# Attention of eight batches and an MLP on one core: later AV products, a third u buffer, early MLP products, and keys split by DMA

The chip is one Trainium2 chip, of which the kernel uses **one core**. The metric is the device time of one execution in microseconds (us), as the median of several executions. The word *span* is the time from the first to the last instruction in one profiled execution; in every execution of this case the device time was 1.7 to 1.8 us above its span.

## The reference, cut to what matters

```python
# q, k, v: (8 batches, 8 heads, 576 positions, 64); bias_table: (32, 8)
scores = scale * np.matmul(q, k.transpose(0, 1, 3, 2)) + bias     # bias by distance and head
attn = softmax(scores)                                            # over the keys
x = np.matmul(attn, v).transpose(0, 2, 1, 3).reshape(4608, 512)
h = x @ w_in                                                      # 512 -> 2048
s = np.sin(alpha * h)
g = h + s * s / (alpha + 1e-09)
out = g @ w_out                                                   # 2048 -> 512
```

The kernel works batch by batch (t = 0 to 7). It computes the attention of a batch, two heads ("a pair", p = 0 to 3) at a time, and then one block of 512 tokens of the MLP, whose second half is slipped between the next batch's scores.

## The kernel before: the parts that matter

A scheduler written in Python places "tasks" on the engines at build time. A task has possible engines, predecessors, buffers and a priority (a lower number goes first); an engine then runs its instructions in the order in which they were placed. `NBUF` holds the number of buffers of each kind, and `u` is the exponentials of one pair.

```python
NBUF = {"sc": 4, "av": 2, "mo": 2, "u": 2, "g": 2, "s16": 3, "sq": 3, "outs": 5, "xn": 3}
AV_PRI = 250
# ... (cut)
def load_kqT(t):                      # batches 2 to 7; all of it in SyncE's queue
    nc.sync.dma_start_transpose(out=kraw[:, :, :], in_=staged_k.ap()[t])
    kz = kzs[t % 2]
    nc.sync.dma_start(out=kz[0:64, :, 0:S], in_=kraw[0:64, :, :])
    nc.sync.dma_start(out=kz[64:128, :, S : 2 * S], in_=kraw[64:128, :, :])
    for z in range(2):
        r = slice(64 * z, 64 * z + 64)
        nc.sync.dma_start(out=kts[t % 2][r, :, r], in_=kraw[r, :, 512:S])
    nc.sync.dma_start_transpose(out=qTs[t % 2][:, :, :], in_=staged_q.ap()[t])
# ... (cut)
def plan_tr(t, p, kq, pri, nb, deps=()):    # batches 0 and 1: TensorE transposes a pair
    # ... (cut: transposition into a PSUM buffer c.v of kind "mo")
    def cp(e):                              # copies on VectorE or ScalarE
        if kq == 1:
            put(qTs[t][:, p, :], slice(0, 128))
        else:
            put(kzs[t][:, p, 0:S], slice(0, 64))
            put(kzs[t][:, p, S : 2 * S], slice(64, 128))
    def tail(e):                            # "corners": keys 512 to 575 of both heads
        for z in range(2):
            r = slice(64 * z, 64 * z + 64)
            nc.vector.tensor_copy(
                out=kts[t][r, p, r], in_=kzs[t][r, p, S * z + 512 : S * z + S])
# ... (cut)
def first(t=t):                             # called at the first score of batch t
    if 1 <= t < T - 1:
        load_v16(t + 1)
        load_kqT(t + 1)
    if t + 2 < T:
        stage_kq(t + 2)
```

`kz` holds a pair's keys with the other head's half left at zero, so that a product over 128 rows gives one head alone; `kt` holds the last 64 keys of both heads. `kraw` is the place where a transposed batch lands before it is spread to `kz` and `kt`. There is one `kraw`.

The softmax here doesn't subtract the row's maximum and nothing guards it: scores larger than these inputs give would overflow.

## Time and profile before

| | before |
|---|---|
| median of 3 executions | 414.31 us (414.13 to 416.89) |
| profiled execution | 412.09 us, span 410.3 us |
| TensorE busy | 395.4 us, 96% of the span |
| ScalarE, VectorE busy | 337.3 and 289.7 us |

The kernel is bound by TensorE: its row of busy tenths is 9 from the fifth slice to the last but one. Only time in which TensorE waits or runs cold can be won.

### The profile page before, as it was taken

What the parts mean: (1) busy time and instruction counts of PE and PEld (TensorE: products, weight loads), DVE (VectorE), ACT (ScalarE), POOL (GpSimd) and SP (SyncE); (2) the same over time, 40 slices, a digit from 0 to 9 for tenths busy, and PEclk for the clock granted to TensorE, in tenths of its full rate; (3) what the DMA queues carried; (4) which work ended last, traced back from release to release, by engine and by line L of the source; (5) the groups of instructions that cost most, each with busy time, mean ns of one, the idle gap of its engine ahead of it and who ended that gap; (6) DMA issues with size and microseconds to landing.
All of it is one profiled execution on the core that took longest, in us unless ns stands there. A gap on an engine that the chain in (4) does not pass through costs nothing.

```text
span 410.3 us, 8747 instructions
## 1 busy us (share of the span) xinstructions
PE 395.4 (96%) x3519; PEld 227.5 (55%) x3519; DVE 289.7 (71%) x683; ACT 337.3 (82%) x502; POOL 85.6 (21%) x98
## 2 busy tenths in 40 slices
PE   4897999999999999999999999999999999999996
PEld 1474446754576447744665467645764477444442
DVE  5895996749666976688576956696768766799200
ACT  2877988879988998889888998799979988899311
POOL 7863952044000900071004400120000000000000
PEclk9999999999999999999999999999999999999999
DMA  9899999949900995099906990293000000000111
GB/s 170 189 206 219 205 162 158 216 89 164 185 28 29 155 182 94 27 135 165 131 28 104 161 142 27 69 169 79 27 28 27 26 27 27 28 1 0 53 77 77
DMA packets 135145, 41.90 MB, mean 102 GB/s; under 512 B 121209, under 2 KB 129489, under 8 KB 135105
## 3 DMA queue, kind: packets, MB, share of 16 engines
q0 software_dynamic: 89872, 19.04, 54.5%
q1 hardware_dynamic: 45008, 22.26, 24.2%
q8 instruction: 27, 0.44, 0.4%
q14 instruction: 14, 0.11, 0.1%
q10 hardware_dynamic: 224, 0.05, 0.1%
HBM read 37.76 MB, written 16.52 MB: 132 GB/s over the span
## 4 chain that ended last, share of the span: by engine, by line
PE 88%; DVE 8%; DMA 1%; ACT 1%; issue 1%; ACTq 0%; DVEq 0%
PE sc L408 44%; PE mo L408 30%; PE av L408 11%; PE av L688 2%; DVE kz L496 2%; DVE g L741 2%; DMA phi_sb<-phi_const 1%; DVE u L635 1%; DVE xn L678 1%; DVE qT L496 1%; ACT u L606 1%; DVE kt L542 1%; DVE sq L736 0%; PE mo L507 0%; PE mo L513 0%
## 5 line engine op out<-in xcount | busy, mean ns | idle before, releaser
L606 ACT ACTIVATE u<-sc 128x768 f16<-128x768 f32 (+1 forms) x224 | 165.9, 788 | 28.6 <-PE sc L408 23.5
L408 PE MATMUL mo<-w_out,g 128*128 128x512 f16 x576 | 156.5, 379 | 0.0
L408 PE MATMUL sc<-xT,w_in 128*128 128x512 f16 x576 | 131.2, 379 | 0.5 <-DVE g L741 0.5
L741 DVE SCALAR_TENSOR_TENSOR g<-sq,inv_a,sc 128x512 f16<-128x512 f16 x144 | 104.7, 747 | 7.8 <-ACT sq L734 4.9
L727 ACT ACTIVATE s<-sc,alphaT 128x512 f16<-128x512 f32 x144 | 92.4, 677 | 8.4 <-PE sc L408 7.3
L408 PE MATMUL sc<-qT,kz 128*128 128x192 f16 (+1 forms) x512 | 89.5, 288 | 2.0 <-ACT qT L494 0.7
L408 PEld LDWEIGHTS <-w_in 128*128 128x128 f16 x576 | 55.3, 98 | 64.7 <-issue 0.8
L635 DVE TENSOR_TENSOR u<-u,m2r 128x512 f16<-128x512 f16 (+1 forms) x192 | 70.5, 388 | 17.4 <-ACT u L606 14.9
L408 PEld LDWEIGHTS <-g 128*128 128x128 f16 x576 | 55.8, 98 | 45.2
L408 PEld LDWEIGHTS <-u 128*128 128x128 f16 x1440 | 55.2, 97 | 10.6 <-ACT u L606 2.5
L352 POOL DMA_DIRECT2D v<-in_v_dram x24 | 22.2, 1064 | 163.7 <-PE av L408 163.7
L408 PE MATMUL av<-v,u 128*128 128x65 f16 x1280 | 54.9, 193 | 0.5 <-DVE u L635 0.5
L408 PEld LDWEIGHTS <-kz 128*128 128x128 f16 x512 | 42.6, 98 | 22.0 <-issue 4.4
L734 ACT ACTIVATE sq<-s 128x512 f16<-128x512 f16 x79 | 49.4, 629 | 2.3
L677 DVE RECIPROCAL rd<-av 128x6 f32<-128x6 f32 x64 | 12.0, 188 | 38.1 <-PE av L408 38.1
L408 PE MATMUL av<-vh,u 128*128 128x130 f16 x160 | 35.2, 220 | 0.1
L678 DVE TENSOR_TENSOR xn<-av,rd 128x384 f16<-128x384 f32 x64 | 31.4, 491 | 2.2
L736 DVE TENSOR_TENSOR sq<-s 128x512 f16<-128x512 f16 x65 | 27.3, 421 | 2.9 <-ACT s L727 2.5
L496 DVE COPY outs<-mo 128x512 f32<-128x512 f32 x27 | 18.6, 690 | 10.9 <-PE mo L408 10.7
L688 PEld LDWEIGHTS <-xn 128*128 128x128 f16 x160 | 13.6, 98 | 18.0 <-DVE xn L678 6.4
L494 ACT ACTIVATE outs<-mo 128x512 f32<-128x512 f32 x9 | 5.4, 597 | 20.7 <-PE mo L408 20.7
L688 PE MATMUL av<-id_sb,xn 128*128 128x128 f16 x160 | 19.5, 220 | 2.9 <-DVE xn L678 2.8
(68 smaller groups left out, 185.6 us busy)
## 6 DMA issues: line engine op xcount, KB each, us to landing
out_dram<-outs SPq DMA_DIRECT2D x36, 256.0 KB, 2.0
staged_k<-in_k_dram POOLq DMA_DIRECT2D x6, 576.0 KB, 11.2
staged_q<-in_q_dram POOLq DMA_DIRECT2D x6, 576.0 KB, 17.5
kz<-kraw SPq DMA_DIRECT2D x12, 288.0 KB, 7.0
v<-in_v_dram POOLq DMA_DIRECT2D x24, 128.0 KB, 6.0
w_in<-in_moe_w_in_dram POOLq DMA_DIRECT2D x4, 512.0 KB, 8.5
w_out<-in_moe_w_out_dram POOLq DMA_DIRECT2D x4, 512.0 KB, 10.8
w_out<-in_v_dram SPq DMA_DIRECT2D x4, 256.0 KB, 9.1
```

Source lines behind the costliest of these rows:

```text
L352: nc.gpsimd.dma_start(out=vs[t % 2][:, c, :, 0:D], in_=vp[128 * c : 128 * c + 128],)
L408: nc.tensor.matmul(out=out, lhsT=lhsT, rhs=rhs, start=start, stop=stop)
L496: k_of(e).tensor_copy(out=o, in_=i)
L606: nc.scalar.activation(out=o, in_=x, func=AF.Exp, scale=0.125)
L635: nc.vector.tensor_tensor(out=io, in0=io, in1=m2[:, 2 * p : 2 * p + 2, x0 : x0 + hi - lo], op=ALU.mult,)
L677: nc.vector.reciprocal(out=r, in_=a[:, :, :, D])
L678: nc.vector.tensor_tensor(out=xn.v[:, 0:nq].rearrange("p c (z d) -> p c z d", z=2), in0=a[:, :, :, 0:D], in1=r.unsqueeze(3).to_broadcast([ ...
L688: nc.tensor.transpose(out=tr.v[:, qc - q0 : qc - q0 + 128], in_=xn.v[:, i], identity=id_sb)
L727: nc.scalar.activation(out=s16.v, in_=h.v, func=AF.Sin, scale=alphaT[:, f : f + 1])
L734: nc.scalar.activation(out=sq.v, in_=s16.v, func=AF.Square)
L736: k_of(e).tensor_tensor(out=sq.v, in0=s16.v, in1=s16.v, op=ALU.mult)
L741: nc.vector.scalar_tensor_tensor(out=gcell[b].v[:, f, :], in0=sq.v, scalar=inv_a[:, f : f + 1], in1=h.v, op0=ALU.mult, op1=ALU.add,)
```

## The change

The intent is to shorten the first 60 us, where TensorE waits for ScalarE and VectorE. It has three parts. **Part 1**: the AV products (exponentials times v) of batch 0 get a late priority, so that the next pair's scores go first, and `u` gets a third buffer (it shares its memory with `nat1`, where inputs of batch 0 are loaded). **Part 2**: the first MLP products are cut in two, so that three of four need not wait for the last pair. **Part 3**: keys of pairs 2 and 3 of batch 0 and of all pairs of batch 1 leave PSUM in one 128-partition copy to `kraw`, and four DMAs spread them from there. These DMAs go into SyncE's queue. The placing times `T_TR1` of batch 1's transpositions also change, from 38.5 and 38.5 to 33 and 37 (among the lines cut below).

```diff
-NBUF = {... "u": 2, ...}
+NBUF = {... "u": 3, ...}
-AV_PRI = 250
+AV_PRI = (2000, 250)
+FAR = 1
   ... (cut)
@@ plan_tr
+        far = kq == 0 and (t == 1 or p > FAR)
+            elif far:
+                put(kraw[:, p, :], slice(0, 128))
-        eng = {"DVE": 0.75, "ACT": 0.72} if kq else {"DVE": 1.6, "ACT": 1.55}
+        eng = {"DVE": 0.75, "ACT": 0.72} if kq or far else {"DVE": 1.6, "ACT": 1.55}
+        if far:
+            farq.append((p, x))
+            if t and p % 2 == 0:
+                return [], []
   ... (cut)
+            def split(e):
+                kz = kzs[t]
+                nc.sync.dma_start(out=kz[0:64, p0:p1, 0:S], in_=kraw[0:64, p0:p1, :])
+                nc.sync.dma_start(out=kz[64:128, p0:p1, S : 2 * S], in_=kraw[64:128, p0:p1, :])
+                for z in range(2):
+                    r = slice(64 * z, 64 * z + 64)
+                    nc.sync.dma_start(out=kts[t][r, p0:p1, r], in_=kraw[r, p0:p1, 512:S])
+            y = plan.add({"DMA": D_SPLIT}, split, [z[1] for z in ps_], pri)
@@ plan_av
-            prev = [plan.add({"PE": 0.31}, mm, us + prev, base + AV_PRI + i,
+            prev = [plan.add({"PE": 0.31}, mm, us + prev, base + AV_PRI[t > 0] + i,
@@ plan_moe_in
-            m = plan.add({"PE": 4 * t_pe(512)}, mm, xs, pri, nb=T_W if b == 0 else 0.0, new=[hb])
+            if b == 0 and f < 4:
+                m = plan.add({"PE": 3 * t_pe(512)}, lambda e, mm=mm: mm(e, range(3)), xs012,
+                             pri - 100, nb=T_W, after=qk_last[:], new=[hb])
+                m = plan.add({"PE": t_pe(512)}, lambda e, mm=mm: mm(e, range(3, 4)), xs + [m],
+                             pri, use=[hb])
+            else:
+                m = plan.add({"PE": 4 * t_pe(512)}, mm, xs, pri, new=[hb])
```

More of the change, by code (lines that the diff above doesn't have):

```diff
@@ L34 @@
 LAT = {"PE": 0.2, "ACT": 0.18, "DVE": 0.18, "POOL": 0.2, "DMA": 0.0}
-NBUF = {"sc": 4, "av": 2, "mo": 2, "u": 2, "g": 2, "s16": 3, "sq": 3, "outs": 5, "xn": 3}
+NBUF = {"sc": 4, "av": 2, "mo": 2, "u": 3, "g": 2, "s16": 3, "sq": 3, "outs": 5, "xn": 3}
 class Task:
@@ L94, in run @@
     def run(self, t0):
-        free = {e: t0 for e in ("PE", "ACT", "DVE", "POOL")}
+        free = {e: t0 for e in ("PE", "ACT", "DVE", "POOL", "DMA")}
         todo = list(self.tasks)
@@ L163 @@
 T_V = (18.5, 45.0)
-T_TR1 = (38.5, 38.5)
+T_TR1 = (33.0, 37.0)
+D_SPLIT = 3.5
 T_W = 30.0
@@ L172 @@
 SIN_SET = "trig_and_small"
-SLACK = {"PE": 0.02, "ACT": 0.02, "DVE": 0.02, "POOL": 0.02}
+SLACK = {"PE": 0.02, "ACT": 0.02, "DVE": 0.02, "POOL": 0.02, "DMA": 0.0}
 def _bucket_table(max_abs: int) -> np.ndarray:
@@ L282 @@
     nat2 = nat2x[0:SN, 0 : 2 * H * SI * D].rearrange("s (kq h x) -> s kq h x", kq=2, h=H)
-    nat1x = sgl.tile([128, 2 * (H - 2) * SI * D], F16, name="nat1")
-    nat1 = nat1x[0:SN].rearrange("s (kq h x) -> s kq h x", kq=2, h=H - 2)
+    ubs = [sgl.tile([128, 9 * S], F16, name=f"u{i}") for i in range(3)]
+    uit = [0]
+    nat1 = ubs[2][0:SN, 0 : 2 * (H - 2) * SI * D].rearrange("s (kq h x) -> s kq h x", kq=2, h=H - 2)
     def new_g():
@@ L289, in new_u @@
     def new_u():
-        return tp.tile([128, 9, S], F16, name="u", tag="u", bufs=NBUF["u"])
+        uit[0] += 1
+        return ubs[(uit[0] - 1) % 3].rearrange("p (c q) -> p c q", c=9)
     def new_xn():
@@ L496, in copy_on @@
             k_of(e).tensor_copy(out=o, in_=i)
+    farq, split_of = [], {}
     def plan_tr(t, p, kq, pri, nb, deps=()):
         b, c = Buf("mo"), Cell()
+        far = kq == 0 and (t == 1 or p > FAR)
         def mm(e):
@@ L537, in plan_tr @@
             return [x], [x]
+        if far:
+            farq.append((p, x))
+            if t and p % 2 == 0:
+                return [], []
+            ps_ = [y for y in farq]
+            farq.clear()
+            p0, p1 = ps_[0][0], ps_[-1][0] + 1
+            def split(e):
[6 more added lines that the diff above has]
+            y = plan.add({"DMA": D_SPLIT}, split, [z[1] for z in ps_], pri)
+            for z in ps_:
+                split_of[(t, z[0])] = y
+            return [y], [y]
         def tail(e):
@@ L563, in plan_alpha @@
         return plan.add({"DVE": 0.4}, cp, [m], 5000, use=[b])
+    qk_last = []
     def plan_pair(t, p, kqt, tails, first, gate, ub):
@@ L612, in plan_pair @@
             head = head or [m]
+            qk_last[:] = [m]
             x = plan.add({"ACT": t_act(n)}, ex, [m] + gate, base + 20, use=b + [ub])
@@ L709, in plan_moe_in @@
         gcell[b], gbuf[b] = Cell(), Buf("g")
+        xs012 = [d for w in range(2) for d in xdone[(0, w)][0 : NP - 1]]
         xs = [d for t in range(T) for w in range(2) for d in xdone.get((t, w), [])
@@ L715, in plan_moe_in, with mm @@
             h, s16, sq = Cell(), Cell(), Cell()
-            def mm(e, f=f, h=h):
-                h.v = new_sc(1)
-                for j in range(4):
+            def mm(e, js=range(4), f=f, h=h):
+                if js[0] == 0:
+                    h.v = new_sc(1)
+                for j in js:
                     full(
@@ L815 @@
             tails = tr[(t, p, 0)][1] if t < 2 else []
+            if (t, p) in split_of:
+                kqt, tails = kqt + [split_of[(t, p)]], []
             u, done = plan_pair(t, p, kqt + pe_gate, tails, first, gate, ub)
```

## The prediction

> **What bounds the kernel now.** I read the page first: shares, slices, and the chain that ended last.
>
> ```profile
> span 410.3 us, 8747 instructions
> PE 395.4 (96%) x3519; PEld 227.5 (55%) x3519; DVE 289.7 (71%) x683; ACT 337.3 (82%) x502; POOL 85.6 (21%) x98
> ...
> PE   4897999999999999999999999999999999999996
> ...
> PE 88%; DVE 8%; DMA 1%; ACT 1%; issue 1%; ACTq 0%; DVEq 0%
> ```
>
> TensorE fills nearly every slice, so only time in which it waits can be won. Adding up its matmuls from the built program (columns over 2.4 GHz plus 2.5 ns each) gives 384.9 us; some 25 of the 410.3 us are losses, most of them before 100 us. So next I read the busy time by stretch of 5 us (PE is the second number) and the timeline of ScalarE.
>
> ```profile
> 20.00:25.00 5.00, 4.34 (x67) 3.17 (x65) 4.90 (x15) 3.77 (x7) 5.00 (x8) 1.00 1.03 203
> ...
> 35.00:40.00 5.00, 3.15 (x56) 2.17 (x53) 2.19 (x7) 2.97 (x5) 1.51 (x2) 1.00 1.20 242
> ...
> 55.00:60.00 5.00, 4.48 (x21) 2.04 (x21) 4.88 (x14) 4.78 (x8) 1.74 (x1) 1.00 2.45 158
> ...
> 23.66 0.81 ACT L606 ACTIVATE u<-sc 128x768 f16<-128x768 f32 x1 [1.19 <-PE sc L408]
> ...
> 35.82 0.81 ACT L606 ACTIVATE u<-sc 128x768 f16<-128x768 f32 x1 [0.65 <-PE sc L408]
> ...
> 39.62 1.31 ACT L494 ACTIVATE kz<-mo 64x576 f16<-64x576 f16 x2
> 40.96 2.04 ACT L727 ACTIVATE s<-sc,alphaT 128x512 f16<-128x512 f32 x3
> ...
> 58.64 1.28 ACT L789 ACT_TABLE_LOAD   x1
> ```
>
> The first batch's attention ends near 39; its exponentials stop for TensorE (1.19 us when pair 2 needs a u buffer that pair 0's AV still reads). From 41 to 58.6 ScalarE and VectorE are both full: first MLP half, with batch 1's key copies in between. That is what the change is after. It also puts new work on the SyncE queue, so I read that queue's own timeline, and TensorE's where pair 2 of batch 1 starts:
>
> ```profile
> 57.81 5.83 SPq L340 DMA_TRANSPOSE kraw<-staged_k  x1
> 69.33 0.63 SPq L342 DMA_DIRECT2D kz<-kraw  x1
> 70.07 1.25 SPq L343 DMA_DIRECT2D kz<-kraw  x1
> 71.37 1.32 SPq L346 DMA_DIRECT2D kt<-kraw  x2
> 72.80 6.35 SPq L347 DMA_TRANSPOSE qT<-staged_q  x1
> 79.25 8.80 SPq L782 DMA_DIRECT2D out_dram<-outs  x4
> ...
> SPq L340 <- DMA staged_k<-in_k_dram: 44.2, 1, 44.2
> ...
> 72.49 0.81 PE L408 MATMUL sc<-qT,kz 128*128 128x384 f16 x4
> ```
>
> This is the load of batch 2: SyncE sits 44.2 us on the staged keys, and is not free for anything else until 79.25. Before, that harmed nobody.
>
> **What the Trainium skill says.** "DMA: Bandwidth & Descriptors", section on the anatomy of one DMA: DMA engines do not wait on semaphores; the wait is on the issuing sequencer, before dispatch. The trace agrees: the 44.2 us are SyncE's, and the key copies behind stay behind it. "TensorE: Matmul & The Clock Gate", Part 2 (step by step): only weight loads are pulled ahead, matmuls stay in program order; so a score that waits holds all later TensorE work. No wait before is long enough to show it. The same page, Part 1 (what's actually happening): after about 3.4 us idle the array is at 1.2 GHz, and warm again after some 3.4 us of work. The trace has the cold start: four 128x384 matmuls took 1.56 us at 10.14 and 0.82 us at 23.08.
>
> **The change, part by part.**
>
> 1. *Third u buffer, AV of batch 0 at a late priority.* In the built order TensorE now sends pair 2's scores before the last AVs of pair 0. It removes the ScalarE waits of 1.19, 0.74 (at 27.35) and 0.65: 2.6 us. Last exponential 36.63 - 2.6 = 34.0; the tail from there to the last xT copy took 39.57 - 36.63 = 2.9, so attention ends near 37.
>
> 2. *First MLP products without the last pair.* Nine of the first sixteen matmuls (at 0.216 us: 1.9 us) now lie in the AV tail. The two key copies on ScalarE (1.31 us) no longer stand before the first sine: it comes near 37.3 instead of 40.96, 3.6 us earlier.
>
> 3. *Keys through one 128-partition copy.* A pair cost two 64x576 copies of 0.76 us and two corner copies of about 0.18; now one 128x576 copy of 0.76 (same length: a qT copy of that shape took 0.76). In the MLP stretch of batch 0 this frees on VectorE 3 x 0.76 + 1.4 = 3.7 us and gives it two or three squares (0.4) in exchange; ScalarE's 17.7 us (40.96 to 58.64) falls to 16 sines at 0.67, 8 squares at 0.52 and 4 copies at 0.53 = 17.0. Gain 0.7. Parts 1 to 3: 4.3 us, so batch 1's scores begin near 55 instead of 59.13.
>
> 4. *The split by DMA, in the SyncE queue.* The built order of SyncE is: batch 1 pairs 0-1 split (four DMAs); transpose of batch 2's keys into kraw; four copies out of it; transpose of batch 2's queries; only then batch 1 pairs 2-3 split. TensorE's first weight load of batch 1 pair 2 waits for exactly that DMA (I compared semaphore and count in the built program). Timing from the lines above: staged keys landed at 57.8, SyncE free at 79.25. First half issued from 79.25, second to 80.5. Landing: the output DMA issued at 79.25 took 4.2 us, the key copies issued at 69 to 70 took 6.4 and 8.8; with half their bytes I take 5 for both, so 85. Two extra splits (0.33 MB each, at some 0.2 MB per us in a DMA system busy from 20 to 57) push the staged keys by up to 3 us; I take 1.5. Pair 2 can start at **86.5**.
>
> TensorE gets there far earlier: pairs 0-1 took 72.49 - 59.13 = 13.4, less the six second-MLP matmuls that the new order puts later (1.3), from 55: near 67. It **stands still about 19 us**. Parts 1 to 3 end before that and do not count at all: neither staging of batch 2 nor SyncE's transposes wait for them.
>
> 5. *From there to the end.* Before, 410.3 - 72.49 = 337.8 us for matmuls that sum to 330.9: 6.9 over. The new order has 333.5 us from this place (twelve more matmuls). 333.5 + 6.9 = 340.4. Everything after is TensorE-bound, with no slack to catch up. Cold clock: 3.4 to 4 us at half speed, 2 us lost.
>
> Sum: 86.5 + 340.4 + 2 = 428.9 span. The median of the timed runs was 4.0 above the profiled span (414.3 against 410.3); partly the profiled execution being quick itself (412.1). I take 3: **432 us**, 4% slower.
>
> The order also has a defect: batch 2's keys overwrite kraw before pairs 2-3 of batch 1 are read from it, so heads 4 to 7 of batch 1 see wrong keys. The scores are tiny; worked out on the host this moves the output by 0.35% in norm, which a tolerance will likely pass. It costs no time.
>
> **Rivals.**
>
> - *No stall; the change works as meant.* Then 410.3 - 4.3 = 406 span, 410 us, -1%. For it: such a stall would be glaring to whoever made the change, and its own scheduler counts a split as 3.5 us. Against: SyncE issues in order, and the same transposes occupied it to 79.25. For this the staged keys would have to land 20 us sooner; GpSimd stages them at 45.44, behind loads that the change does not touch.
> - *The split is late in batch 0 already.* kraw of pair 2 is copied near 16.3, four issues at about 0.65 us and 4 to 7 us of landing put it at 21 to 24; ScalarE wants it at 22.5. This can eat 1.5 of part 1's 2.6 us: 411 to 412 us without the stall, and nothing with it, as the stall's end is not set by TensorE.
> - *VectorE becomes the bound of batch 0's attention.* From 18.6 it has about 17.6 us of masks and norms, so ends no earlier than 36.2: parts 1 and 2 then give 3 us, not 3.6. Again hidden by the stall.
> - *The stall is shorter or longer.* Landing after 4.2 us, no delay of the staging, warm clock: 83.5 + 340.4 + 3 = 427. Delay 3.5, landings 8.8, cold for longer: 91.5 + 340.4 + 3 + 4 = 439.
>
> **Range and chances.** The last rival's ends, a little wider below as 6.9 may shrink: 425 to 439. Same needs the stall to be 10 us shorter than worked out: 5%. Faster needs both no stall and twice the gain: 1%.
>
> **What would show it.** Busy time by stretch: TensorE nearly idle from about 67 to 86, one wait of 15 to 20 us at a score matmul (the helper's line is 412 in the new kernel), put down to a DMA kz<-kraw; matmuls after it at double length for some 4 us and a PEclk digit below 9. SyncE's timeline: the split of kz at 79 to 82, right after the query transpose. Part 1: no ScalarE gap near 23. Part 2: first sine near 37. Part 3: no 64x576 copies after 20 us. It is wrong if pair 2 of batch 1 starts before 75; if it starts at 86 but the end is below 424, the rest was not TensorE-bound as I take it.

## The result, and the profile after

The changed kernel took **426.83 us** (425.97 to 427.34, 4 runs) and the kernel before, in the same rounds, 414.22 us (410.79 to 416.89, 4 runs). The ratio of the fast runs is 1.031, with a 95% interval of 1.023 to 1.039: slower. Here and below a ratio is the mean time of one kernel's fast runs over the mean of the other's fast runs of the same rounds, so it is not quite the ratio of the medians.

First the page of the changed kernel, with the same lines as in the prediction and the slices of the granted clock:

```profile
span 425.5 us, 8795 instructions
...
PE 395.3 (93%) x3518; PEld 227.7 (54%) x3518; DVE 285.7 (67%) x668; ACT 335.8 (79%) x499; POOL 86.0 (20%) x98
...
PE   6889982099999999999999999999999999999996
...
PEclk9999998589999999999999999999999999999999
...
PE 79%; DMA 14%; POOL 5%; issue 1%; ACT 0%; SPq 0%; POOLq 0%; ACTq 0%
```

TensorE is busy for as long as before (395.3 against 395.4 us), but the row of slices has a hole, 2 and 0, where before it was full. The clock row falls to 8 and 5 in these two slices and is 8 in the next, and the chain that ended last now runs through DMA for 14% of the span. So 15 us were added as waiting, not as work. The busy time by stretch of 5 us shows the hole (columns: the stretch, then busy time of TensorE, of its weight loads, of VectorE, ScalarE and GpSimd with counts, granted clock, DMA share, GB/s). First one stretch of the kernel before, where TensorE is full:

```profile
70.00:75.00 5.00, 5.00 (x72) 3.73 (x71) 3.77 (x12) 4.43 (x7) 0.00 (x0) 1.00 2.20 184
```

Then the changed kernel:

```profile
65.00:70.00 5.00, 1.77 (x37) 1.37 (x34) 1.67 (x6) 1.94 (x3) 0.33 (x1) 1.00 1.62 123
70.00:75.00 5.00, 0.00 (x0) 0.00 (x0) 0.00 (x0) 0.00 (x0) 0.00 (x0) 0.55 2.43 157
75.00:80.00 5.00, 0.00 (x0) 0.00 (x0) 0.00 (x0) 0.00 (x0) 0.00 (x0) 0.50 1.87 219
80.00:85.00 5.00, 0.72 (x2) 0.24 (x3) 0.00 (x0) 0.00 (x0) 0.00 (x0) 0.50 0.85 166
85.00:90.00 5.00, 5.00 (x40) 2.81 (x39) 1.64 (x5) 3.13 (x5) 0.00 (x0) 0.74 0.14 52
```

TensorE stands still from 66.8 us, VectorE and ScalarE from 68.2 and 67.6, and all of them until 84; GpSimd has nothing to do in this time either. TensorE's timeline says what it waited for (columns: start, length, engine, line, operation, and the idle time before with what ended it):

```profile
84.28 0.96 PE L412 MATMUL sc<-qT,kz 128*128 128x384 f16 x2 [17.51 <-DMA kz<-kraw]
85.04 1.49 PE L412 MATMUL mo<-w_out,g 128*128 128x512 f16 x3
...
93.18 0.81 PE L412 MATMUL mo<-w_out,g 128*128 128x512 f16 x3
```

One wait of 17.51 us, at a score of pair 2 of batch 1, for `kz<-kraw`. The three 128x512 products right after it take 1.49 us, and 0.81 us at 93.18: the cold clock. SyncE's own timeline shows why the DMA was late:

```profile
59.10 5.80 SPq L344 DMA_TRANSPOSE kraw<-staged_k  x1
...
75.01 6.33 SPq L351 DMA_TRANSPOSE qT<-staged_q  x1
81.39 0.60 SPq L557 DMA_DIRECT2D kz<-kraw  x1
...
84.04 20.76 SPq L822 DMA_DIRECT2D out_dram<-outs  x4
```

The splits (lines 557 to 561 of the new kernel) stand behind the load of batch 2: keys' transpose, four copies, queries' transpose. Issued at 81.39, the split landed after 2.85 us, and TensorE started.

ScalarE's timeline answers to the lines on parts 1 and 2:

```profile
21.02 4.42 ACT L637 ACTIVATE u<-sc 128x768 f16<-128x768 f32 x6 [0.72 <-PE sc L412]
...
37.35 1.84 ACT L761 ACTIVATE s<-sc,alphaT 128x512 f16<-128x512 f32 x3 [0.54 <-PE sc L412]
```

The gap of 1.19 us at 23.66 is gone, and the first sine comes at 37.35 instead of 40.96. Of these 3.6 us, 1.4 are chance: this execution's first exponential started at 9.66 instead of 11.09, since its first loads landed sooner. So about 2.2 us of gain were there, and the stall swallowed them.

### The profile page after: what moved, and what is told of

The parts are those of the page before. It is cut to its first block, busy times and chain, and to the rows that moved or that the text cites. A ratio compares the mean times of both kernels' runs of the same rounds, so it can differ in the third digit from the quotient of the medians.

```text
span 425.5 us, 8795 instructions
## 1 busy us (share of the span) xinstructions
PE 395.3 (93%) x3518; PEld 227.7 (54%) x3518; DVE 285.7 (67%) x668; ACT 335.8 (79%) x499; POOL 86.0 (20%) x98
## 4 chain that ended last, share of the span: by engine, by line
PE 79%; DMA 14%; POOL 5%; issue 1%; ACT 0%; SPq 0%; POOLq 0%; ACTq 0%
PE sc L412 40%; PE mo L412 28%; PE av L412 9%; DMA staged_q<-in_q_dram 8%; DMA v1st<-in_v_dram 4%; PE av L720 2%; POOL v L376 1%; DMA natx<-in_q_dram 1%; DMA kz<-kraw 1%; POOL w_in L391 1%; POOL kz L402 0%; POOL vh L379 0%; POOL kz L401 0%; POOL m2r L426 0%; POOL nat L386 0%
## 5 line engine op out<-in xcount | busy, mean ns | idle before, releaser
L412 PE MATMUL sc<-qT,kz 128*128 128x192 f16 (+1 forms) x512 | 90.7, 290 | 21.6 <-DMA kz<-kraw 17.9
L709 DVE RECIPROCAL rd<-av 128x6 f32<-128x6 f32 x64 | 12.1, 189 | 38.5 <-PE av L412 38.3
```

The costliest lines, as they stand in the source:

```text
L412: nc.tensor.matmul(out=out, lhsT=lhsT, rhs=rhs, start=start, stop=stop)
```

## The experiments

Two theories came first. **Theory Q (the queue)**: the loss is the place of batch 1's second split in SyncE's queue, and nothing else. **Rival L (the landing)**: the split by DMA is slow in itself, because it lands late, whatever its place. (The recorded texts call these theory A and rival B; their rival C is that the new order of TensorE costs time as well.) Later two questions followed: where the expected gain went once the stall is gone, and which part is worth what.

The table gives one row per kernel. Stages are read from ScalarE's timeline of the profiled execution, whose loads of the activation table mark the changes between exponentials and sines: attention 0 from the first exponential to the next load, MLP 0 from there to the load after, attention 1 from there to the load after that. "Load at" is the time of that last load; from there to the very last table load every kernel takes 262.6 to 265.3 us. One execution is one sample: the first exponential alone varies from 9.0 to 11.7 us.

| kernel | median us (range) | ratio to before, 95% | first exp. | attention 0 | MLP 0 | attention 1 | load at | span |
|---|---|---|---|---|---|---|---|---|
| before | 414.22 (410.79 to 416.89) | | 11.09 | 25.56 | 21.99 | 26.96 | 85.60 | 410.3 |
| after | 426.83 (425.97 to 427.34) | 1.031 | 9.66 | 23.95 | 20.32 | **45.38** | 99.31 | 425.5 |
| e1_load_after_split | 412.53 (408.41 to 414.60) | 0.995 (0.989 to 1.000) | 11.40 | 28.37 | 20.40 | 27.75 | 87.92 | 412.8 s |
| e2_queries_after_split | 424.19, one run | | 11.38 | 28.18 | 20.39 | 37.55 | 97.50 | 422.4 |
| e3_split_batch0_only | 418.16 (410.47 to 418.46) | none | 10.45 | 30.10 | 24.29 | 26.68 | 91.52 | 416.6 s |
| e4_no_split | 416.70 (410.19 to 417.67) | 0.996 (0.988 to 1.004) | 11.39 | 23.83 | **27.65** | 27.95 | 90.82 | 415.5 s |
| e8_corners_from_psum | 411.39 (409.09 to 411.86) | 0.992 (0.986 to 0.998) | 10.11 | 26.13 | 20.31 | 26.04 | 82.59 | 407.3 |
| e9_before_corners_from_psum | 416.64 (414.62 to 417.45) | 1.004 (0.999 to 1.010) | 11.72 | 27.08 | 21.91 | 27.65 | 88.36 | 414.8 |
| e10_no_split_corners_psum | 412.40 (411.20 to 415.62) | 0.996 (0.988 to 1.003) | 10.89 | 29.52 | 23.93 | 26.17 | 90.51 | 413.8 |
| e12_mlp_whole | 410.98 (409.87 to 411.65) | 0.991 (0.984 to 0.997) | 10.75 | 28.21 | 21.09 | 25.66 | 85.71 | 409.9 |
| e11_av_early | 411.01 (410.22 to 411.80) | 0.990 (0.986 to 0.994) | 9.61 | 29.24 | 20.28 | 26.49 | 85.62 | 409.0 |
| e13_split_pair3 | 415.91 (413.41 to 416.29) | 1.000 (0.996 to 1.005) | 9.03 | **34.41** | 20.84 | 26.18 | 90.46 | 414.0 |
| **e14_split_batch1_only** | **407.31** (405.43 to 408.58) | **0.981** (0.977 to 0.985) | 10.52 | 24.01 | 20.90 | 25.79 | 81.22 | 405.4 |
| e15_best_av_early | 409.28 (408.04 to 409.94) | 0.985 (0.980 to 0.989) | 11.20 | 26.59 | 20.01 | 25.07 | 82.87 | 407.8 |

An "s" marks a profiled execution that counted as slow, because it was over 1.5% above the fastest of its kernel. The kernel before ran 410.8 to 420.4 us in these rounds, so a single profile can flatter or harm a kernel by some us. The ratios rest on fast runs. For e3 all runs but one counted as slow and no ratio was given. The profiled executions of e1, e4 and e10 are among the slowest of their kernels, and that of e8 is its quickest (409.09). All outputs passed the comparison.

### e1: the same DMAs, another order

```diff
     def qk(e, ...):                       # scores of pair p of batch t
+        if t == 1 and p == 2:
+            load_kqT(2)
     def first(t=t):
-            load_kqT(t + 1)
+            if t > 1:
+                load_kqT(t + 1)
```

> The change as it is, but SyncE issues the load of batch 2's keys and queries after the split of batch 1's pairs 2-3, not before. Theory A (order of the SyncE queue): the same DMAs through the same queue, so the wait of 17.5 us at pair 2's first score falls under 1 us, PEclk stays full, span 404 to 407, time 407 to 410 us. Rival B (the split itself lands late because the DMA engines are busy): a wait of 5 us or more stays, span above 411. Rival C (the stall is only part of it, the new order of TensorE costs too): no wait, but span above 410.

SyncE's queue and the TensorE waits of this kernel:

```profile
59.66 0.59 SPq L557 DMA_DIRECT2D kz<-kraw  x1
...
71.65 6.07 SPq L344 DMA_TRANSPOSE kraw<-staged_k  x1
```

```profile
25.42 0.34 PE L412 MATMUL sc<-qT,kz 128*128 128x384 f16 x1 [1.85 <-DMA kz<-kraw]
...
27.01 0.34 PE L412 MATMUL sc<-qT,kz 128*128 128x384 f16 x1 [1.25 <-DMA kz<-kraw]
```

The split of batch 1 is issued at 59.66 in place of 81.39, the stall at its pair 2 is gone, and attention 1 falls from 45.38 to 27.75 us. No DMA was removed or shortened. That decides for theory Q on the 17.5 us. By the letter of the expectation, though, this is rival C's outcome: no wait there, but a span of the profiled execution of 412.8 us, far above what I expected. Its trace shows a second loss, in batch 0. TensorE waits there 1.85 and 1.25 us for the split of batch 0, whose key copies landed 7.5 and 8.6 us after issue, and attention 0 takes 28.4 us. In this execution the landing, rival L's point, is the loss of batch 0. The waits cost twice here, as the same kernel's busy time by stretches of 1 us shows (the clock is third from the end):

```profile
24.00:25.00 1.00, 0.00 (x0) 0.00 (x0) 0.86 (x3) 0.42 (x1) 0.47 (x1) 1.00 1.08 221
...
28.00:29.00 1.00, 1.00 (x9) 0.47 (x6) 0.44 (x2) 0.19 (x1) 0.76 (x1) 0.50 1.07 223
```

TensorE is idle at 24, still at full clock; at 28 it is busy, at half clock. From 27 to 31 the granted clock was 0.75, 0.50, 0.50 and 0.54, with TensorE always busy: 0.25 + 0.50 + 0.50 + 0.46 = 1.7 us lost on top of the 3.1 us of waits. In e8 below, waits of 0.30 and 2.20 us left the clock at 1.00.

The changed kernel has the same code in batch 0, and did not lose this: its profiled execution took 23.95 us there. Its split went out sooner and landed sooner (after 5.4 and 5.0 us). First the changed kernel, then e1:

```profile
14.63 0.53 SPq L557 DMA_DIRECT2D kz<-kraw  x1
```

```profile
17.84 0.53 SPq L557 DMA_DIRECT2D kz<-kraw  x1
```

So the split of batch 0 can be late, and in some executions is not. The new order also mends a defect: in the changed kernel batch 2's keys overwrite `kraw` before the split of pairs 2 and 3 of batch 1 has read it.

### e2: half of the queue moved

```diff
 def load_kqT(t):
     # ... keys as before
-    nc.sync.dma_start_transpose(out=qTs[t % 2][:, :, :], in_=staged_q.ap()[t])
+    if t != 2:
+        load_qT(t)                        # batch 2: called at pair 2 of batch 1
```

> The change, but of batch 2's load only the transpose of the queries is issued after the split; the keys' transpose and copies stay before it. Theory A: the split is issued 6.3 us sooner (75 instead of 81.4), so the wait at pair 2 is about 11 us instead of 17.5 and the span about 419. If what counts were the landing of something else (staged keys, load of the DMA engines), the wait would not move by this amount. The order of the keys is still wrong, so heads 4 to 7 of batch 1 are off as in the change.

```profile
75.50 0.63 SPq L561 DMA_DIRECT2D kz<-kraw  x1
...
79.46 2.99 SPq L355 DMA_TRANSPOSE qT<-staged_q  x1
```

```profile
81.25 0.83 PE L416 MATMUL sc<-qT,kz 128*128 128x384 f16 x2 [8.46 <-DMA kz<-kraw]
```

With only the queries' transpose taken from ahead of it, the split is issued 5.9 us earlier (75.50), as theory Q wants. TensorE starts 3.0 us earlier (81.25 against 84.28), not 5.9: the split now takes 5.5 to 5.7 us to land, probably because other transfers run beside it (157 GB/s from 75.0 to 75.5 us), where it took 2.85 us in the quiet end of the stall (68 GB/s from 80 to 81 us). No run tests that. The shorter wait of 8.46 us is partly due to TensorE arriving later. So the dose has the right sign, and less than its full size.

### e3 and e4: which split, and none

```diff
-        far = kq == 0 and (t == 1 or p > FAR)
+        far = kq == 0 and t == 0 and p > FAR      # e3: batch 0 alone
+        far = False                               # e4: no split; parts 1 and 2 stay
```

> The change with the split by DMA in batch 0 alone; batch 1's keys are copied by VectorE and ScalarE in two halves as before. Theory A: no long wait, span 406 to 408 (some 2 us more than with the split of batch 1 in good order, for the 64x576 copies back in the MLP stretch). Rival C: above 410.

> The change without any split: only three u buffers, late AV of batch 0 and early MLP products. Theory A: span 406 to 409. If the split in batch 0 comes late (its copies landed 8.5 us after issue in the changed kernel, and ScalarE waited 0.72 us at 21.0), this equals or beats the run with the split in batch 0 alone; if the 128-partition copy is worth something there, it is about 1 us slower.

Neither has a stall in batch 1 (26.7 and 27.95 us), as theory Q wants. e3 has a long attention 0 (30.1 us), as e1 has; e4 has the shortest of all, 23.83 us. So **a late split in batch 0 can eat what part 1 gives**; stage lengths of two slow executions do not prove it, and e14 below tests it on fast runs. But in e4 MLP 0 takes 27.65 us. VectorE's timeline and GpSimd's show a surprise:

```profile
45.13 4.34 DVE L571 COPY kt<-kz 64x64 f16<-64x64 f16 x2
```

```profile
44.82 2.22 POOL L338 DMA_DIRECT2D staged_k<-in_k_dram  x1 [0.42 <-issue]
46.54 2.72 POOL L338 DMA_DIRECT2D staged_q<-in_q_dram  x1
```

Two corner copies took 4.34 us together, one of them 4.13 us, where the median of the sixteen is 0.18 us. The long one lasts as long as GpSimd generates the staging DMAs. The Trainium skill, "SBUF — State Buffer", section "Who interferes with whom", says that a VectorE copy in a two-port mode and GpSimd exclude each other for a whole instruction, and that the blocked one stands still. The trace agrees: the copy ends at 49.5, just after the second staging issue (49.3), and TensorE waited 3.75 us for the `g` behind it. In the kernel before, the longest of these copies took 0.59 us. This rests on one execution, marked slow: two of e4's six runs took 410.2 and 411.0 us, and their traces were not kept.

### e8, e9, e10: the corners taken from PSUM

The same skill, "VectorE: DVE Perf Modes", section "Why PSUM operands drop a tier", says that PSUM has only one read port for VectorE, so a copy from there cannot enter a two-port mode. If the lock is the cause, a corner copy from the transposition's PSUM buffer should never be long.

```diff
         for z in range(2):
             r = slice(64 * z, 64 * z + 64)
-            nc.vector.tensor_copy(out=kts[t][r, p, r],
-                                  in_=kzs[t][r, p, S * z + 512 : S * z + S])
+            o = kts[t][r, p, r]
+            nc.vector.tensor_copy(out=o[:, 0:4], in_=pin[r, 85, 2:6])
+            nc.vector.tensor_copy(out=o[:, 4:64].rearrange("d (p i) -> d p i", i=SI),
+                                  in_=pin[r, 86:96])
```

e8 has this edit on e1, e9 on the kernel before, e10 on e1's order with `far = False`.

> The repaired order (batch 2's load after the split), and the two corner copies of batch 0's pairs 0 and 1 read PSUM instead of the keys in SBUF. In the run with the repaired order alone those copies took 1.99 us for two at 15.0 (median elsewhere 0.18 each), while GpSimd was writing descriptors and casting; they stand before the copy whose split pair 2 waits for. Theory D (VectorE's SBUF-to-SBUF copies are held up by GpSimd and so delay the split): no corner copy over 0.4 us, kraw of pair 2 copied by 16, wait for the split at pair 2 of batch 0 under 1.5 us instead of 3.1, first exponential to first table load 25 us or less instead of 28.4; time 407 to 411. Rival E (the split is late because of its own landing): the copies get short, but the wait at pair 2 stays 2 us or more.

> The kernel before, with all its corner copies read from PSUM: nothing else. Theory D: corner copies never over 0.4 us in any run; the time moves little where the copies happened not to be held up, so 412 to 416, with a smaller spread of the runs than before's 410.8 to 418.9. If the spread of before comes from something else, it stays.

> Three u buffers, late AV, early MLP products, no split by DMA, corner copies from PSUM. Theory D: the stretch between the first two table loads, 27.7 us in the run without a split (a corner copy of 4.1 us in it, at 45.1, beside the staging of batch 2 by GpSimd), falls to about 22; first exponential to first table load stays near 24; time 408 to 411. If the 4.1 us had another cause, it stays at 25 or more.

In e8 and e9 no corner copy took more than 0.22 us, and in e10 MLP 0 fell from 27.65 to 23.93 us (expected: about 22): the long copies are gone, as the lock would have it. No run isolates the lock from other effects of the edit. The gain on the clock is small, though. e8's ratio is 0.992, but attention 0 still takes 26.1 us and TensorE still waits for the split:

```profile
24.46 0.34 PE L412 MATMUL sc<-qT,kz 128*128 128x384 f16 x1 [2.20 <-DMA kz<-kraw]
```

The split was issued from 16.41 on, and its key copies landed after 5.5 and 7.4 us. So with short corner copies there still is a wait of 2.5 us, and the landing is what it waits for. e9 is not faster than before, and its attention 0 is not shorter; its runs only spread less (2.8 us in six, against 5.8 in the nine fast runs of before). e10's attention 0 of 29.5 us was a miss against my 24: from the traces I take it that the corners now hold the PSUM buffer that the next transposition wants, but no run tests that alone, and the profiled execution (415.62) was over 3 us slower than the other three.

### e13: less split in batch 0

```diff
-FAR = 1
+FAR = 2          # on e8: only pair 3 of batch 0 goes by DMA
```

> Repaired order, corners from PSUM, but in batch 0 only pair 3 goes by DMA. Theory E: pair 3 has 5 us more than pair 2, so a landing of 8 us is hidden and there is no wait for a kz DMA in batch 0; first stretch 24 to 25.5 us; time 407 to 410. A wait at pair 3 of more than 1 us would speak for a DMA system still too busy.

```profile
34.20 0.34 PE L412 MATMUL sc<-qT,kz 128*128 128x384 f16 x1 [2.74 <-DMA kz<-kraw]
```

This was a miss, and it settles little. The scheduler placed pair 3's copy into `kraw` late (at 27.60 us), so the split was issued at 28.38, landed 5.8 and 6.0 us later, and was late again; attention 0 took 34.4 us. It did not give the landing more slack, which was its purpose.

### e14: the split where there is slack, and only there

```diff
-FAR = 1
+FAR = 3          # on e1: batch 0's keys stay with VectorE, corners from SBUF
```

> Repaired order, split by DMA for batch 1 alone, batch 0's keys copied by VectorE as in the kernel before (corners from SBUF). In the repaired runs TensorE waited 2.5 to 3.5 us for the split of batch 0's pair 2, which landed 7 to 8.6 us after issue. Theory E (the split is a loss in batch 0 because its landing is longer than the time pair 2 has): no such wait, first exponential to first table load 24 us (23.8 in the run without any split) instead of 26.1 to 28.4; between the first two table loads 20.4 as in all runs with batch 1 split; time 406 to 410, at or below the run with corners from PSUM. If it is not the split of batch 0, that first stretch stays at 26 or more.

The kernel's busy time in the stretch where the changed kernel fell into its hole:

```profile
65.00:70.00 5.00, 5.00 (x58) 3.35 (x57) 3.14 (x11) 4.31 (x7) 1.12 (x1) 1.00 1.88 185
```

TensorE is full there, and no wait for a DMA into `kz` is left. Attention 0 (24.0 us) is as short as in e4, MLP 0 (20.9) nearly as short as in the changed kernel, attention 1 (25.8) shorter than before. e14 differs from e1 in `FAR` alone, and the intervals of their ratios (0.977 to 0.985, 0.989 to 1.000) do not overlap (the two ran on different chips, each beside its own runs of before): on fast runs too, leaving batch 0's keys to VectorE pays. No corner copy took longer than 0.52 us: those of batch 1, which lay beside the staging, are DMAs now. The kernel takes **407.31 us, 1.9% less than before** (ratio 0.981). It is the fastest, and beats both kernels.

### e12, e11 and e15: what parts 1 and 2 are worth

```diff
-            if b == 0 and f < 4:
+            if False:                    # e12, on e8: part 2 undone
-AV_PRI = (2000, 250)
+AV_PRI = (250, 250)                      # e11 on e8, e15 on e14: part 1 undone
```

> As the run with repaired order and corners from PSUM, but the first MLP products whole, after the last pair (part 2 undone). By the prediction part 2 is worth about 1 to 2 us: first sine that much later after the first table load (3.7 us in the changed kernel; about 5 here), time 1 to 2 us more than the run with it.

> As the run with repaired order and corners from PSUM, but AV of batch 0 at the old priority (part 1 undone but for the third u buffer). The prediction gave part 1 2.6 us of ScalarE waits; but in that run pair 2's scores wait for the split anyway, so putting AV before them should cost little: 0 to 1.5 us against the run with late AV, first exponential to first table load 26 to 27.5 instead of 26.1.

> The version with the split for batch 1 alone, in repaired order, and the AV of batch 0 back at its early priority (part 1 of the change undone, the rest kept). Theory: part 1 is worth 1 to 1.5 us of batch 0's attention where nothing else disturbs it: from the first exponential to the first later load of the activation table I expect some 25.5 us in place of 24.0, and a timed median of 408 to 409.5 in place of 407.3. Rival: part 1 is worth nothing, as the run that undid it in a disturbed version suggests: 24.0 and 407.3, and the 2% of the best version come from parts 2 and 3 in batch 1 alone.

Without part 2 the first sine comes 4.37 us after the table load in place of 3.74, and MLP 0 takes 21.09 us in place of 20.31. The medians, 410.98 and 411.39, show no difference, where I expected 1 to 2 us. By the stage lengths part 2 is worth under 1 us, and the times show nothing of it.

Without part 1's late priority (the third `u` buffer stays), the time of e11 (411.01) does not differ from that of e8 (411.39), perhaps because pair 2's scores have to wait for the late split anyway. In its profile attention 0 took 29.24 us, longer than the 26 to 27.5 expected, but e8's 26.13 comes from its quickest execution. In e15, where nothing disturbs batch 0, the waits at pair 2's place are back. ScalarE's timeline of e15:

```profile
29.13 2.76 ACT L639 ACTIVATE u<-sc 128x576 f16<-128x576 f32 x4 [0.90 <-PE sc L412]
...
36.96 0.81 ACT L639 ACTIVATE u<-sc 128x768 f16<-128x768 f32 x1 [0.64 <-PE sc L412]
```

With one of 0.38 us between them, these are 1.9 us of waits. e14's timeline has none from 24 us to its table load; there it reads:

```profile
25.11 4.55 ACT L639 ACTIVATE u<-sc 128x768 f16<-128x768 f32 x6
```

The median is 409.28 against 407.31, 2.0 us more. These two ran on different chips beside different runs of before (416.2 and 415.24), and the intervals of their ratios overlap. So the waits are shown; that part 1 is worth some 2 us is likely, and not settled.

## Why the prediction was right

The prediction said 432 us with a range of 425 to 439 and slower; measured were 426.83 us. The mechanism was right, and two sizes were off.

- **The stall (part 4) was right.** Foreseen: TensorE arrives near 67 and pair 2 starts at 86.5. Measured: 66.8 and 84.28, a wait of 17.5 us for `kz<-kraw`, right behind the queries' transpose. e1 shows that the queue's order is the cause, e2 that taking a part away moves it. SyncE was free at 81.39, against 80.75 foreseen (79.25 plus my 1.5): staged keys came 1.3 us later than before, and their transpose took longer to land. The term that was mis-sized is **the landing: 5 us assumed, 2.85 measured**. I took it from copies issued while much else was moving; at the end of the stall hardly anything else moves. e2, where more moves, had 5.5 to 5.7. I had also waited for the issue of the split's second copy (some 0.6), and TensorE started on the first. Less the later SyncE (0.6), that makes the 2.2 us between 86.5 and 84.28.
- **The rest (part 5) was right.** From 84.28 to the end there are 425.5 - 84.28 = 341.2 us; foreseen were 340.4 plus 2 for the cold clock. The clock was at 0.50 until about 87.5 us, which cost some 1.6 us. Taken off the 341.2, these and the 333.5 us of matmuls leave 6.1 us over, where the prediction took 6.9.
- **The step from span to median failed.** I added 3 us; measured are 1.3 (426.83 - 425.5). The 4.0 us of before were 1.8 us that every execution has, and the luck of one quick profile among executions that differ by 6 us. The stall seems to take that luck away: the chain that ended last reaches the split through staging and SyncE, not through batch 0's attention, and the four executions of the changed kernel lie within 1.4 us. These two terms, 2.2 and 1.7 us, with 1.2 on the rest, are nearly the whole of the 5.2 us that separate 432 from 426.83.
- **Parts 1 and 2 came in kind and did not count.** The gap at pair 2 was gone and the first sine came at 37.35 (foreseen 37.3). That this fits so well is luck: 1.4 us of the 3.6 were an early start, and 2.2 were the change. Batch 1's scores began at 53.1 to 55.1 (foreseen 55). MLP 0 shrank from 21.99 to 20.32 us, more than my 0.7 for part 3, since the sines also start sooner. e14 and e15 make part 1's worth likely some 2 us of my 2.6; e12 leaves under 1 us for part 2.
- **The rival of the late split in batch 0** was right in kind and too small. I gave it 1.5 us. In the changed kernel's own profile it was a wait of ScalarE of 0.72 us; in e1, attention 0 took 28.4 us where e4, without any split, took 23.8. The waits of 3.1 us and the 1.7 us lost to the clock after them are about that difference of 4.5 us.
- **Two readings were loose.** VectorE was not full from the start of the first MLP half (3.48 of 5 us from 40 to 45). And the cold start was read from lengths alone (1.56 against 0.82 us): the granted clock of that profile is 1.00 from 10 to 15 us.
- **What I did not see** is that the corner copies, once moved, may meet GpSimd's staging. In the changed kernel, where batch 1's corners are DMAs, the longest took 1.37 us, in batch 0 and ahead of the stall; in the kept execution of e4 it was 4.13 us.

Left open: why the key copies of pair 2 in batch 0 land after 5.0 us (changed kernel) to 9.4 us (e2). Other transfers run then, but no run took them away. Open too is whether that time can be shortened, and what SyncE does during the 6.33 us of a transpose.

## What to carry to other kernels

Before moving work to a DMA, read the queue in which it will be issued, in order: a transfer costs what stands before it, and a wait at the head of the queue is everyone's. A gain ahead of a stall is worth nothing, so find where the next fixed point in time is before adding up savings. A landing time is to be taken from a moment as busy as the one in question, and the split by DMA pays only where the data is wanted more than that much later (batch 1, not batch 0).

## What the Trainium skill lacked or had wrong

- "DMA: Bandwidth & Descriptors" gives, for one DMA issued by GpSimd, some 2 us of fixed cost plus the bytes at 436 GB/s, by which I estimate 2.3 us for 144 KB. A 144 KB copy from SBUF to SBUF landed after 2.85 us when little else moved, and after 5.5 to 5.7 us in e2; copies of 72 KB issued at 14 to 21 us took 5.0 us (changed kernel, pair 2) to 11.7 us (e2, pair 3). The page has no figure for such a copy issued by SyncE, or for its landing beside other traffic.
- The same page, on DMA transposes, does not say how long one of this size holds the issuing queue. Here SyncE was held 2.2 to 8.8 us by one transpose of a batch's keys or queries (576 KB), and 0.60 us by a plain copy of 144 KB.
- "TensorE: Matmul & The Clock Gate" puts the cold clock after some 3.4 us of idleness. The stall of 17.5 us agrees: the granted clock fell to 0.50 at 70.5, 3.7 us after the last matmul, and was full again at 88, some 4 us after the first. But in e1 the clock fell to 0.50 although no wait was longer than 1.85 us: two waits, with one matmul of 0.34 us between them, were enough. Later in e1, waits of 0.64 and 1.27 us (to 61.3 us) brought it to 0.50 from 62 to 65, while in the changed kernel the same two waits (to 55.1 us) left it at 1.00. The page speaks of idle windows and, elsewhere, of short gaps that make the clock swing; it does not say how much work a window may hold and still count as idle.
- "SBUF — State Buffer" has the lock between VectorE and GpSimd, and tells of a 6.8-fold slowing of VectorE. If the lock is the cause here, it was 23-fold: a 64x64 copy of 0.18 us became one of 4.13 us beside two issues of staging DMAs.
